# A RetNet front and an MLP-mixer on one core: letting the first front's PSUM tiles come from either of two bank sets

## The chip, the cores and the metric

One core of a Trainium2 chip runs the whole kernel. The metric is the device time of one execution in microseconds (us). Five executions of the kernel before are given by their median; one further execution was profiled.

## The reference

The kernel computes a recurrent retention layer over q, k and v (4 batches, 8 heads, 768 positions, head size 64) and feeds it to an MLP-mixer block with a token part and a channel part.

```python
state = gamma * state + k[:, :, t] (outer) v[:, :, t]      # per batch and head
y[:, :, t] = scale * q[:, :, t] @ state
...
x = y.transpose(0, 2, 1, 3).reshape(B, S, H * D)            # (4, 768, 512)
u = x + (relu(x.T @ w_tok1) @ w_tok2).T                     # w_tok1 (768, 256), w_tok2 (256, 768)
out = u + relu(u @ w_ch1) @ w_ch2                           # w_ch1 (512, 1536), w_ch2 (1536, 512)
```

All inputs and the output are float32; the matmuls run on float16 tiles.

## The kernel before

**Work.** A batch is cut into four *pairs* of heads, p = 0 to 3 (128 of the 512 columns each), and the sequence into six chunks of 128 positions, three to a half. `front(b, p)` makes one pair of one batch, `back(b)` the channel part of one batch. Line numbers are those of the kernel before.

`front(b, p)` records these operations, each with the engine that runs it:

- loads: k as float32 (`kf`, L261), q and v; for batches 0 and 1 on POOL's DMA queue with a cast to float16 (L280, L283, L286), but k of the very first pair on SP's; for batches 2 and 3 all on SP's queue with casts on POOL (L298);
- the scaling of k on DVE (L317); the transposes of k and q on PE (L333, L337, here "Tk" and "Tq") and their copies out of PSUM (L345; kT on DVE and qT on ACT for batch 0); from batch 2 on they are DMA transposes on SP (L352);
- the products of k and v on PE (L366), the running state U on DVE (L375, L378), its scaled copies r on ACT and DVE (L385, L392);
- the scores, half by half (L408 on PE, two PSUM tiles to a half), masked on DVE (L421), or, for pairs 1 to 3 of batch 0 (second head of each), cast on ACT (L419) and masked by a select on POOL (L425);
- the outputs Y (L442 and L445 on PE), scaled into x (L456 on ACT, L460 on DVE) and cast to float16 on POOL (L473) or, for pair 3 of batch 0, directly by ACT;
- the token part: L496 (with wt1), relu on ACT (L504), L517 (with wt2), the addition to x on DVE (L524), the cast to float16 ("u", L535) on POOL, and the transpose of u into uT: on PE and ACT for batch 0 (L548, L557), as a DMA transpose on SP for the others (L571).

`back(b)` runs `ch1` (L604 on PE with wc1, relu L617 on ACT) and `ch2` (L637 on PE with wc2, addition L646 on DVE, store L653 on SP) for each half: 96 L604 and 72 L637 matmuls in a batch (the last tile of the last batch in two parts). An accumulator of ch1 takes four L604, one for each pair.

**Order.** Nothing is scheduled by hand. Every operation is an `Op` with an engine, a priority, an occupancy and a latency in ns, what it depends on, and the buffers (`Slot`) it takes and uses. `arrange()` plays these costs forward: it takes, again and again, the operation that can start first (with ties by priority; PE prefers fronts to backs), and the resulting list is the program order of every engine. The engines then run their lists in order and wait on semaphores. So a buffer that `arrange()` sees as taken moves an operation back in the order, and the order stays even where the buffer comes free earlier on the chip.

**Buffers.** Each `Slot` names one tag, and `BUFS` says how many buffers a tag has. All PSUM tiles are 128 x 512 float32: five with the tag "fa" for the fronts, three with "ba" for the backs. In batch 0 the token part of pairs 0 and 1 (`TOKBA = 2`) uses "ba", which the backs do not need by then; all else of a front uses "fa".

```python
BUFS = dict(kf=4, qf=4, vf=4, k16=3, q16=4, v16=4, kT=4, qT=4, U=3, am=8, x16=2, h1=4, u16=3, u16w=2,
            x=3, uT=3, h2=2, o=3, r16=NR, fa=5, ba=3)
```

**DMA in the plan.** `arrange()` keeps a clock for SP's ring and one for POOL's (`free["SPring"]`, `free["POOLring"]`). After the first 5 us it lets a transfer of SP begin only when POOL's ring is free.

**Zero matmuls.** Where the plan has PE wait before it takes a PSUM tile in batch 0's front, `tile_of` (L198) puts matmuls on a tile of zeros there, as many as fill three quarters of the planned wait. They write into the tile that is being taken.

Of the kernel before, what the change touches and what calls it, by code (L numbers as in the profile page):

```python
# [17 lines left out]
def kernel(  # L18
# [64 lines left out]
    r16 = [const_p.tile([P, NC - 1, P], F16, name=f"r16_{i}") for i in range(NR)]  # L83
    for t in r16:
# [9 lines left out]
    BUFS = dict(kf=4, qf=4, vf=4, k16=3, q16=4, v16=4, kT=4, qT=4, U=3, am=8, x16=2, h1=4, u16=3, u16w=2,  # L94
                x=3, uT=3, h2=2, o=3, r16=NR, fa=5, ba=3)
    SEM, GUARD = 80, 100
# [3 lines left out]
    QLONG = 1200  # L100
    ASIDE, RACT = ((1, 1), (1, 3), (2, 1), (2, 3), (3, 1), (3, 3)), ()
    KPOOL = ()
    FILL, TOKBA, PRE, TWICE, SOFT = 0.75, 2, 2, 1, 2
    ops = []

    class Slot:


        def __init__(self, tag):
            self.tag, self.users, self.tile = tag, [], None  # L110

    class Op:
        def __init__(self, eng, prio, occ, lat, emit, deps=(), takes=(), uses=(), guard=0, dma=0):
# [9 lines left out]
    def arrange():  # L123


        way = {}
        for op in reversed(ops):
            if op.first is not None:
                way[op] = way.get(op, 0) + op.lat + SEM
                for d in op.deps:  # L130
                    way[d] = max(way.get(d, 0), way[op])
        for op in ops:
            if op.first is not None:
                op.prio = (op.prio[0], 0, EARLY * op.first - way[op], op.first)
        free = dict(PE=5700, ACT=5000, DVE=4600, POOL=1100, SP=1300, SPring=1300, POOLring=1300)
        taken = {t: [] for t in BUFS}
        todo, order, ring = list(ops), [], dict(SP=[], POOL=[])
        while todo:
            best = []
            for op in todo:  # L140
                if any(d.end is None for d in op.deps):
                    continue
                start = free[op.eng]
                if op.dma and len(ring[op.eng]) >= RING[op.eng]:
                    start = max(start, ring[op.eng][op.count - 1 - RING[op.eng]])
                for d in op.deps:
                    if d.eng == op.eng and (d.dma or d.eng == "PE"):
                        continue
                    start = max(start, d.end + (30 if d.eng == op.eng else SEM) + op.guard)
                more = {}  # L150
                for s in op.takes:
                    q = taken[s.tag]
                    n = len(q) + more.get(s.tag, 0) - BUFS[s.tag]
                    more[s.tag] = more.get(s.tag, 0) + 1
                    if n >= 0:
                        old = q[n]
                        if any(u.end is None for u in old.users):
                            break
                        start = max([start] + [u.end + SEM for u in old.users])
                else:  # L160
                    best.append((start, op))
            t = min(b[0] for b in best)

            eng = min(best, key=lambda b: (b[0], b[1].prio))[1].eng
            start, op = min((b for b in best if b[1].eng == eng and b[0] <= t + 20),
                            key=lambda b: b[1].prio)
            free[op.eng] = start + op.occ
            op.start = start
            if op.dma:

                mine, other = op.eng + "ring", ("POOL" if op.eng == "SP" else "SP") + "ring"
                at = max(free[mine], start + (op.occ + 200 if op.eng == "POOL" else 50))
                both = max(0, free[other] - at)
                shared = min(op.dma, both // 2)
                if op.eng == "SP" and at > 5000:

                    at, shared = max(at, free[other]), 0
                free[mine] = at + op.dma + shared
                free[other] += shared
                op.end = free[mine] + 1600  # L180
                ring[op.eng] += [op.end if op.eng == "POOL" else free[mine]] * op.count
            else:
                op.end = start + op.lat
            for s in op.takes:
                taken[s.tag].append(s)
            todo.remove(op)
            order.append(op)
        return order
# [33 lines left out]
    def front(b, p):  # L222
        first = b == 0
        g = 0 if first else GUARD
        n = [0]

        def op(eng, occ, lat, emit, deps=(), takes=(), uses=()):
# [95 lines left out]
        KT, QT = Slot("kT"), Slot("qT")  # L323

        def turn(src, dst, dep, eng):
            T = Slot("fa")

            def emit():
                T.tile = tp = tile_of(T, ps, [P, 512], FP).bitcast(F16)
                for c in range(NC):  # L330
                    if src is Q and soft and b < LONG:
                        for j in range(2):
                            nc.tensor.transpose(tp[j * D:(j + 1) * D, c * P:(c + 1) * P],  # L333
                                                src.tile[:, j * NC + c], ident16)
                        continue
                    o = src.tile[:, c] if src is K else src.tile[:, 2 * c:2 * c + 2]
                    nc.tensor.transpose(tp[:, c * P:(c + 1) * P], o.rearrange("p h d -> p (h d)"), ident16)  # L337
            t = op("PE", 340, 500, emit, [dep, t1_done.get(b * NP - 1) if b > 0 else None], [T], [src])

            def emit():  # L340
                d, o = tile_of(dst, sb, [P, S], F16), T.tile[:, :S]
                if dst is QT and b < LONG:
                    d = d.rearrange("d (f p i) -> d f i p", f=2, i=HC)
                    o = o.rearrange("d (f i p) -> d f i p", f=2, i=HC)
                (nc.scalar.copy if eng == "ACT" else nc.vector.tensor_copy)(d, o)  # L345
            occ = dict(ACT=1350 if dst is QT and b < LONG else 700, DVE=470)[eng]
            return op(eng, occ, occ + 90, emit, [t], [dst], [T])

# [8 lines left out]
        qt = crossbar(Q, QT, qc) if b >= XQ else turn(Q, QT, qc, "ACT")  # L357


        ST, US, RS = Slot("fa"), Slot("U"), Slot("r16")  # L360

        def emit():
            st = tile_of(ST, ps, [P, 512], FP)
# [32 lines left out]
        am_ops = []  # L396
        two_before = y_done.get(b * NP + p - 2)
        for hf in range(2):
            A = [Slot("fa"), Slot("fa")]

            def emit(hf=hf, A=A):
                a = [tile_of(A[j], ps, [P, 512], FP).rearrange("p (i t) -> p i t", t=P)
                     for j in range(2)]
                for i in range(HC):
                    t = slice((hf * HC + i) * P, (hf * HC + i + 1) * P)
                    for j in range(2):
                        r = slice(j * D, (j + 1) * D)
                        nc.tensor.matmul(a[j][:, i], KT.tile[r, t], QT.tile[r, t],  # L408
                                         start=True, stop=True)
            a = op("PE", 180, 350, emit, [kt, qt, two_before], A, [KT, QT])  # L410
            for j in range(2):
                off = first and (p, 2 * hf + j) in ASIDE
                M = AM[2 * hf + j]

                def emit(j=j, A=A, off=off, M=M):
                    am = tile_of(M, sb, [P, HC, P], F16)
                    src = A[j].tile.rearrange("p (i t) -> p i t", t=P)
                    if off:
                        nc.scalar.copy(am, src[:, :HC])  # L419
                    else:  # L420
                        nc.vector.tensor_tensor(am, src[:, :HC], mask, ALU.mult)  # L421
                m = op(*(("ACT", 390, 470) if off else ("DVE", 470, 550)), emit, [a], [M], [A[j]])
                if off:
                    def emit(M=M):
                        nc.gpsimd.affine_select(  # L425
                            out=M.tile, in_=M.tile, compare_op=ALU.is_ge, fill=0.0,
                            base=0, pattern=[[0, HC], [1, P]], channel_multiplier=-1)
                    m = op("POOL", 470, 540, emit, [m], [], [M])
                am_ops.append(m)
        X16 = Slot("x16")  # L430
        x_ops, xf = [], []
        for hf in range(2):
            Y = Slot("fa")

            def emit(hf=hf, Y=Y):
                y = tile_of(Y, ps, [P, 512], FP)
                R = RS.tile
# [48 lines left out]
            if not first or p < DIRECT:  # L486
                x_ops.append(op("POOL", 450, 510, lambda e=emit_16: e(False), [ev] + x_ops, tk16, [X] + us16))

        FA = "ba" if first and p < TOKBA else "fa"
        T1, H1 = Slot(FA), Slot("h1")  # L490

        def emit():
            acc = tile_of(T1, ps, [P, 512], FP)
# [4 lines left out]
        t1 = op("PE", 690, 860, emit, x_ops + [wops["t1", 0], None if first else t2_done.get(b * NP + p - 1)], [T1], [X16])  # L498
# [6 lines left out]
        hr = op("ACT", 300, 380, emit, [t1], [H1], [T1])  # L505
        tt, uc = [], None
        wide = b >= XU
        T, UW = Slot(FA), Slot("u16w")
        for hf in range(2):
            T2, U16 = Slot(FA), UW if wide else Slot("u16")  # L510

            def emit(hf=hf, T2=T2):
                acc = tile_of(T2, ps, [P, 512], FP)
# [24 lines left out]
            if wide:  # L538
                continue
            if first:  # L540
                T = Slot(FA)

            def emit(hf=hf, U16=U16, T=T):
                if hf == 0 or first:
# [118 lines left out]
    for p in range(NP):  # L663
        front(0, p)
# [46 lines left out]
```

## Time and profile before

| | us |
|---|---|
| median of 5 runs | 202.94 |
| lowest and highest of them | 201.8 and 203.68 |
| profiled execution | 200.37 |
| its span, first to last instruction | 198.7 |
| PE busy in the span | 191.6 |
| DVE, ACT, POOL busy | 113.5, 92.5, 77.2 |

The span is what the trace covers; 1.7 us of the profiled execution lie around it. The profiled execution was faster than the five by 1.4 us and more, so a sum made from the trace is carried to the median as a difference. The page of the profile gives the span in 40 slices of 5 us: a digit is the share of the slice in which an engine was busy, in tenths. PE counts as busy while matmuls overlap, so its digits say that something was running and not that it ran at its peak. Where a row of a timeline has brackets at its end, the engine was idle before it for so long, and the name in the brackets ended that idle time. A transfer is shown by its issue; the time to its landing is given apart.

### The profile page before, as it was taken

How to read it: one execution, taken by the hardware profiler on the slowest of the kernel's cores; microseconds unless marked ns; L12 is line 12 of the kernel's file. 1: busy time of each engine (PE TensorE's matmuls, PEld its weight loads, DVE VectorE, ACT ScalarE, POOL GpSimd, SP SyncE). 2: the span in 40 equal slices, each digit the busy share in tenths (PEclk: the TensorE clock that was granted, in tenths of full speed). 3: DMA queues.
4: the chain of work that ended last, by engine and by line, in shares of the span. 5: the costliest groups of instructions: out<-in, count | busy, mean ns of one | idle time of the engine just before them, and what ended most of it. 6: DMA issues, size and time to landing. Idle time of an engine off the chain costs nothing.

```text
span 198.7 us, 4693 instructions
## 1 busy us (share of the span) xinstructions
PE 191.6 (96%) x1876; PEld 117.4 (59%) x1876; DVE 113.5 (57%) x285; ACT 92.5 (47%) x207; POOL 77.2 (39%) x124
## 2 busy tenths in 40 slices
PE   7799899999999999999999999999999999999993
PEld 2454796567766555666566655675666545545552
DVE  6699766596489875765885487629762021021021
ACT  7266996886682111284126531553326405504600
POOL 7998899945603621333533333243131000000000
PEclk9999999999999999999999999999999999999999
DMA  6999999999999989999999999999614021012012
GB/s 116 186 216 184 210 223 200 163 205 214 132 168 221 206 216 134 258 258 136 231 224 259 240 180 214 221 235 176 98 62 118 9 101 57 3 53 106 0 53 106
DMA packets 90069, 31.75 MB, mean 160 GB/s; under 512 B 82592, under 2 KB 85920, under 8 KB 90048
## 3 DMA queue, kind: packets, MB, share of 16 engines
q1 hardware_dynamic: 64800, 21.63, 56.5%
q0 software_dynamic: 25248, 9.83, 42.6%
q8 instruction: 14, 0.23, 0.5%
q14 instruction: 7, 0.06, 0.1%
HBM read 26.74 MB, written 6.29 MB: 166 GB/s over the span
## 4 chain that ended last, share of the span: by engine, by line
PE 80%; DMA 8%; POOL 7%; DVE 2%; issue 1%; SPq 0%; POOLq 0%; DVEq 0%
PE ba L637 31%; PE ba L604 28%; DMA wt<-in_moe_w_tok_dram 5%; PE fa L496 4%; PE fa L517 4%; PE fa L408 3%; DMA vf<-in_v_dram 3%; PE fa L445 2%; POOL v L286 2%; PE fa L442 2%; POOL kf L261 2%; PE fa L366 2%; PE fa L337 1%; POOL q L283 1%; POOL u L535 1%
## 5 line engine op out<-in xcount | busy, mean ns | idle before, releaser
L604 PE MATMUL ba<-uT,wc 128*128 128x384 f16 x384 | 69.2, 326 | 0.0
L637 PE MATMUL ba<-wc,h 128*128 128x512 f16 (+1 forms) x300 | 68.1, 371 | 0.0
L617 ACT ACTIVATE h<-ba 128x384 f16<-128x384 f32 x96 | 46.8, 491 | 37.9 <-PE ba L604 37.4
L604 PEld LDWEIGHTS <-wc 128*128 128x128 f16 x384 | 35.4, 98 | 22.1
L637 PEld LDWEIGHTS <-h 128*128 128x128 f16 x300 | 27.6, 98 | 25.7
L646 DVE TENSOR_TENSOR o<-x,ba 128x512 f32<-128x512 f32 (+1 forms) x25 | 16.6, 664 | 40.8 <-PE ba L637 40.7
L421 DVE TENSOR_TENSOR am<-fa,mask 128x384 f16<-128x384 f32 x58 | 30.0, 551 | 3.3 <-PE fa L408 2.8
L473 POOL CAST x<-x 128x384 f16<-128x384 f32 x30 | 15.3, 518 | 26.4 <-issue 17.7
L524 DVE TENSOR_TENSOR x<-x,fa 128x384 f32<-128x384 f32 x28 | 14.7, 551 | 13.1 <-PE fa L517 12.9
L456 ACT ACTIVATE x<-fa,gy 128x192 f32<-128x192 f32 (+1 forms) x42 | 15.0, 424 | 15.2 <-PE fa L445 15.2
L535 POOL CAST u16w<-x 128x384 f16<-128x384 f32 x24 | 11.9, 507 | 25.5 <-DVE x L524 19.9
L378 DVE SCALAR_TENSOR_TENSOR U<-U,gp,fa 128x64 f32<-128x64 f32 x64 | 17.7, 277 | 1.3
L317 DVE TENSOR_SCALAR k<-kf,gk 128x384 f16<-128x384 f32 x32 | 15.2, 517 | 3.7 <-DMA kf<-in_k_dram 3.6
L385 ACT ACTIVATE r<-U 64x320 f16<-64x320 f32 x16 | 7.5, 467 | 17.0 <-DVE U L378 16.9
L504 ACT ACTIVATE h<-fa 128x256 f16<-128x256 f32 x14 | 5.4, 386 | 20.5 <-PE fa L496 20.5
L445 PEld LDWEIGHTS <-am 128*128 128x128 f16 x192 | 12.3, 98 | 3.1 <-DVE am L421 0.2
L445 PE MATMUL fa<-v,am 128*128 128x64 f16 x192 | 13.8, 193 | 0.0
L517 PEld LDWEIGHTS <-wt 128*128 128x128 f16 x192 | 11.9, 98 | 2.6 <-issue 0.2
L198 PE MATMUL fa<-zero 128*128 128x512 f16 x37 | 11.2, 440 | 2.1 <-DVE zero L52 1.3
L496 PEld LDWEIGHTS <-wt 128*128 128x128 f16 x192 | 11.7, 98 | 2.5 <-DMA wt<-in_moe_w_tok_dram 0.6
L442 PE MATMUL fa<-r,qT 128*128 128x128 f16 x80 | 12.2, 220 | 0.0
L517 PE MATMUL fa<-h,wt 128*128 128x128 f16 x168 | 12.0, 219 | 0.0
(61 smaller groups left out, 170.8 us busy)
## 6 DMA issues: line engine op xcount, KB each, us to landing
out_dram<-o SPq DMA_DIRECT2D x23, 256.0 KB, 2.6
kf<-in_k_dram SPq DMA_DIRECT2D x9, 384.0 KB, 5.1
qf<-in_q_dram SPq DMA_DIRECT2D x8, 384.0 KB, 5.1
vf<-in_v_dram SPq DMA_DIRECT2D x8, 384.0 KB, 5.5
kf<-in_k_dram POOLq DMA_DIRECT2D x7, 384.0 KB, 9.4
v<-in_v_dram POOLq DMA_DIRECT2D x8, 192.0 KB, 7.1
wc<-in_moe_w_ch_dram POOLq DMA_DIRECT2D x1, 1536.0 KB, 12.6
wc<-in_moe_w_ch_dram POOLq DMA_DIRECT2D x1, 1024.0 KB, 13.8
```

The lines of the kernel that those rows point to most:

```text
L317: (nc.gpsimd if keng == "POOL" else nc.vector).tensor_scalar(k16[:, :, j, :], src, gk[:, h:h + 1], None, ALU.mult)
L378: nc.vector.scalar_tensor_tensor(U[:, c], U[:, c - 1], gp[:, p:p + 1], o, ALU.mult, ALU.add)
L421: nc.vector.tensor_tensor(am, src[:, :HC], mask, ALU.mult)
L442: nc.tensor.matmul(o, QT.tile[:, c * P:(c + 1) * P], R[:, c - 1], start=True, stop=False)
L445: nc.tensor.matmul(o[:, j * D:(j + 1) * D], AM[2 * hf + j].tile[:, i], V.tile[:, j * NC + c], start=(c == 0), stop=(c == 0 or j == 1))
L473: nc.gpsimd.tensor_copy(X16.tile[:, half(hf)], X.tile[:, half(hf), pc])
L496: nc.tensor.matmul(acc[:, jt * P:(jt + 1) * P], wt1[:, i, jt * P:(jt + 1) * P], X16.tile[:, i], start=(i == 0), stop=(i == NC - 1))
L517: nc.tensor.matmul(acc[:, i * P:(i + 1) * P], wt2[:, jt, t], H1.tile[:, jt], start=(jt == 0), stop=(jt == NJ - 1))
L604: nc.tensor.matmul(acc[:, :SH], w[:, ct, f * P:(f + 1) * P], UT.tile[:, ct, sh * SH:(sh + 1) * SH], start=(ct == 0), stop=(ct == NP - 1))
L617: nc.scalar.activation(H2.tile[:, ft], A.tile[:, :SH], AF.Relu)
L637: nc.tensor.matmul(A.tile[:, :CW], H2.tile[:, ft, i * P:(i + 1) * P], wc2[:, ft, cs], start=(ft == 0), stop=(ft == NF - 1))
L646: nc.vector.tensor_tensor(o[:, :CW], X.tile[:, sh * HC + i, cs], A.tile[:, :CW], ALU.add)
```

## The change

The PSUM tiles of batch 0's fronts may come from "fa" or from "ba". A `Slot` now holds a list of tags, and `arrange()` picks for each tile, at the moment it places the operation, the tag of which a buffer comes free first in the plan (the first named if equal). `FREE = 4` makes this hold for all four pairs of batch 0, in the transposes, the products of k and v, the scores and the outputs Y; in the token part it holds for pairs 0 and 1 (which had "ba" alone), and pairs 2 and 3 keep "fa". Fronts of later batches keep "fa", the backs keep "ba".

A second edit is in the plan's view of the DMA rings: a transfer of SP after the first 5 us no longer waits for all of POOL's ring. It waits only for POOL transfers with a planned length over 1900 ns (the weights), where it would overlap them, and shares time with the others. No DMA is added or removed.

```diff
-    FILL, TOKBA, PRE, TWICE, SOFT = 0.75, 2, 2, 1, 2
+    FREE, FILL, TOKBA, PRE, TWICE, SOFT = 4, 0.75, 2, 2, 1, 2
...
-        def __init__(self, tag):
-            self.tag, self.users, self.tile = tag, [], None
+        def __init__(self, *choice):
+            self.choice, self.tag, self.users, self.tile = choice, None, [], None
...
                 for s in op.takes:
-                    q = taken[s.tag]
-                    n = len(q) + more.get(s.tag, 0) - BUFS[s.tag]
-                    more[s.tag] = more.get(s.tag, 0) + 1
-                    if n >= 0:
-                        old = q[n]
-                        if any(u.end is None for u in old.users):
-                            break
-                        start = max([start] + [u.end + SEM for u in old.users])
+                    when = []
+                    for tag in s.choice:
+                        n = len(taken[tag]) + more.get(tag, 0) - BUFS[tag]
+                        if n < 0:
+                            when.append((0, len(when), tag))
+                        elif all(u.end is not None for u in taken[tag][n].users):
+                            when.append((max(u.end + SEM for u in taken[tag][n].users), len(when), tag))
+                    if not when:
+                        break
+                    at, _, tag = min(when)
+                    start = max(start, at)
+                    more[tag] = more.get(tag, 0) + 1
+                    op.tags.append(tag)
...
                 at = max(free[mine], start + (op.occ + 200 if op.eng == "POOL" else 50))
+                if op.eng == "SP" and at > 5000:
+
+                    for t0, t1 in long:
+                        if at + op.dma > t0:
+                            at = max(at, t1)
                 both = max(0, free[other] - at)
                 shared = min(op.dma, both // 2)
-                if op.eng == "SP" and at > 5000:
-
-                    at, shared = max(at, free[other]), 0
                 free[mine] = at + op.dma + shared
                 free[other] += shared
+                if op.eng == "POOL" and op.dma > 1900:
+                    long.append((at, free[mine]))
...
+        FB = ("fa", "ba") if first and p < FREE else ("fa",)
+        FT = ("fa", "ba") if first and p < TOKBA else ("fa",)
...
-        ST, US, RS = Slot("fa"), Slot("U"), Slot("r16")
+        ST, US, RS = Slot(*FB), Slot("U"), Slot("r16")
...
-            A = [Slot("fa"), Slot("fa")]
+            A = [Slot(*FB), Slot(*FB)]
...
-            Y = Slot("fa")
+            Y = Slot(*FB)
...
-        FA = "ba" if first and p < TOKBA else "fa"
-        T1, H1 = Slot(FA), Slot("h1")
+        T1, H1 = Slot(*FT), Slot("h1")
```

The tile of `turn` becomes `Slot(*FB)` too, and the token part's other tiles become `Slot(*FT)`.

## Prediction

> **What bounds the kernel now.** I read the slices of the page first, then busy time by stretch, then the order of time on PE, POOL and SP.
>
> From the page, then two rows of the busy-time table by stretch (its columns stand in the first line):
>
> ```profile
> PE   7799899999999999999999999999999999999993
> ...
> POOL 7998899945603621333533333243131000000000
> PEclk9999999999999999999999999999999999999999
> ```
>
> ```profile
> core 0: us, PE busy (x) PEld busy (x) DVE busy (x) ACT busy (x) POOL busy (x), PEclk, DMA share, GB/s
> ...
> 22.00:33.00 11.00, 10.66 (x172) 8.91 (x173) 7.02 (x15) 9.75 (x29) 9.78 (x19) 1.00 1.38 214
> ```
>
> There are two regimes. From about 33 us PE is never short: adding matmuls at their spacing (0.163 us for L604, 0.2155 for L637, 0.056 for a 128-column one) gives 162.5 us of work between the first L604 (31.67) and the end of PE (195.5), and the largest gaps between PE rows there are 0.14 to 0.28 us, five in all. Nothing can be won there, only lost; what moves the end is when the front of batch 0 (first 33 us) lets PE start this stream. In the front POOL and ACT, not PE, are full: 9.78 and 9.75 of the last 11 us.
>
> PE in order of time (start, length, row, idle before and its releaser):
>
> ```profile
> 16.49 0.94 PE L408 MATMUL fa<-qT,kT 64*128 64x128 f16 x12
> 17.67 1.89 PE L198 MATMUL fa<-zero 128*128 128x512 f16 x8 [0.25 <-ACT am L419]
> ...
> 22.03 0.84 PE L496 MATMUL ba<-x,wt 128*128 128x128 f16 x12 [0.50 <-DMA wt<-in_moe_w_tok_dram]
> 22.81 0.51 PE L408 MATMUL fa<-qT,kT 64*128 64x128 f16 x12
> 23.25 0.82 PE L198 MATMUL ba<-zero 128*128 128x512 f16 x3
> ...
> 32.78 1.63 PE L604 MATMUL ba<-uT,wc 128*128 128x384 f16 x9
> ```
>
> The first half of pair 2's scores runs with the second half of pair 1's at 16.49; its own second half runs at 22.81, six us later, though qT and kT of pair 2 were there by 16.8. Half a pair's scores take two banks, and five "fa" banks do not reach. PE fills the time with L198 matmuls on zeros. So the bank shortage shows as order, not as waits.
>
> POOL in order of time:
>
> ```profile
> 12.91 0.86 POOL L207 DMA_DIRECT2D wt<-in_moe_w_tok_dram  x1
> 14.07 0.68 POOL L473 CAST x<-x 128x384 f16<-128x384 f32 x1 [0.30 <-ACT x L456]
> ...
> 17.13 0.51 POOL L425 TENSOR_SCALAR_AFFINE_SELECT am<-am 128x384 f16<-128x384 f16 x1 [0.51 <-ACT am L419]
> ...
> 22.78 0.95 POOL L473 CAST x<-x 128x384 f16<-128x384 f32 x2 [0.67 <-ACT x L456]
> ...
> 30.44 2.11 POOL L535 CAST u<-x 128x384 f16<-128x384 f32 x4 [0.35 <-DVE x L524]
> ```
>
> From the issue of wt1 (ends 13.77) to the last u cast (ends 32.55) POOL idles in these four places only, 0.30 + 0.51 + 0.67 + 0.35 = 1.83 us. That is the most a faster front can give as long as POOL's list stays the same.
>
> **The Trainium skill.** "PSUM — Partial Sum Buffer", Specifications (TRN2): eight banks of 2 KiB per partition, out of reach of GpSimd and DMA. The trace agrees on the second: every POOL cast reads and writes SBUF tiles (x<-x), so POOL holds no bank, and the 5 + 3 banks are freed by ACT and DVE. "Perfetto Trace Analysis", Optimizing Tensor Performance: independent groups should rotate through different banks so that evacuation overlaps the next matmuls; the six-us delay above agrees. "TensorE: Matmul & The Clock Gate", What's actually happening: the clock halves after an idle window of about 3.4 us; here it was full in every slice, with 40 zero matmuls as cover. "DMA: Bandwidth & Descriptors", Issuing engines are not separate DMA queues: transfers of SP and POOL interleave on the same 16 engines. So the edit to the planner's ring model changes order only; landings of uT on SP already vary from 2.8 to 7.6 us.
>
> **The change, part by part.** Set beside the old order, the built one shows:
>
> - *Zero matmuls* (L198): 40 become 32. Eight at 0.23 us (10 took 2.32) are 1.8 us of PE, but they stood in waits. I cost them at 0 alone; lower bound 0, upper bound the 1.8. Cover for the clock stays: no stretch of the hand pass leaves PE idle for over 0.7 us.
> - *Scores* (L408): each pair's 12 matmuls now stand together and ahead of the first L496; before, 18 of 48 stood behind it. Follow it by hand, with durations from the rows of before and landing = issue + time to landing. q of pair 1 lands at 4.91 + 5.3 = 10.2. Seven zero matmuls start at 8.45 in a free bank and end at 10.1; Tq1 10.3 to 10.8 (before 11.25), its ACT copy (1.46) ends 12.3, scores 1 at 12.4 (before 14.74 and 16.49). ACT's two casts (0.49 each) end 13.8, so the first POOL select follows the wt1 issue at once. Price: the outputs Y of pair 0 come at 13.3 instead of 12.43 and its x cast at 15.5 instead of 14.07; its reader is L496, which waits for wt1 until 12.91 + 9.1 = 22.0, so this is hidden.
> - Pair 2: q lands 14.05, qT ends 17.2, Y1 waits for r1 on DVE until 16.8, all scores at 17.75. ACT cast done 18.5; POOL is free at 18.1 and idles 0.4. Y2 at 21.2 (before 24.95).
> - Pair 3: q lands 19.06 as before, qT ends 21.5, scores 22.1. The first L496 stands behind them, at 22.75 instead of 22.03: a loss of 0.7 there.
> - From there PE runs L496 2 x 0.67, Y3 0.3, L517 0.67 (its h waits on ACT until 24.85), Y3 0.35, L496 0.67, L517 0.67, and reaches L517 of pair 2 at 28.3. DVE adds (0.56) end 29.35, 29.85, 30.35, 30.85; POOL's last four casts (0.5 each) follow at 29.45 and end at 31.45. A pass with slightly shorter waits on ACT and DVE ended at 31.1.
> - *POOL*: the same casts, selects and DMA issues (17 us of work after wt1), with selects ahead of x casts. kf of batch 1 is issued at 19.5 (before 19.41), so it lands near 33.2 as before. The order puts 27 L604 (4.4 us) ahead of that load's transpose, which before had 12: PE reaches it at 35.6 and does not wait.
> - *SP and POOL ring model*: SP's transfers are now planned to wait for POOL's long ones only. No instruction comes or goes. The first output store moves ahead of the four loads of batch 2 (kf at 54.93 before); it is ready near 58.3, so these loads go 3.4 us later. v of pair 0 lands near 66.1 as the third of them, its cast ends 67, and L366 reads it at 69: cover 2 us, so I cost it at 0; from 0 to +1 if that cover goes.
> - *Later order*: counted from the first L604, batch 1's fronts stand about 2 us of PE work later, ch1 and ch2 about 1.2 us earlier. PE is full either way: 0.
>
> Sum: the stream resumes after the last u cast, at 32.78 before and at 31.35 to 31.7 after, with three L604 done in both: 1.1 to 1.4 us less; I take 1.2. The profiled execution was 200.37 (span 198.7 and 1.7 around it), so it would be 199.2. The median of the five runs is 202.94, 2.6 above that execution; 202.94 - 1.2 = 201.7. Bounds from both sides: at most 1.8 from POOL's idle time; downwards the front may gain nothing, or lose the 0.7 of the later L496.
>
> **Rivals.** A measurement of this kernel can tell about 0.5% (1.0 us) from no change.
>
> *A, the likeliest, 0.58:* the front ends 0.9 to 1.8 us earlier and the stream keeps it: 201.1 to 202.0, mostly more than 0.5%.
>
> *B, 0.24:* the front is held by what does not change (landings of q3 at 19.06 and wt1 at 22.0, POOL full behind them). For: ACT and POOL at 9.8 of 11. Against: POOL's 1.83 us idle. Gain 0 to 0.9: 202.0 to 202.9.
>
> *C, slower, 0.18:* the end of batch 1's front now meets its ch1. Before, on SP:
>
> ```profile
> 73.54 2.76 SPq L571 DMA_TRANSPOSE uT<-u16w  x1
> ```
>
> This last transpose of batch 1 landed 4.7 us after its issue, at 78.24, 7.4 us after its L517 started (70.86). Its first reader came 10.9 us after that start. In the new order between them stand L517 0.67, 22 L637 4.74, L408 0.44, 2 L637 0.43, 6 L604 0.98, Y 0.3 and 3 L604 0.49: 8.05 us. Margin 0.65. If the transpose takes the 7.6 us that another did, PE stalls 2.2 us and the sum is 202.94 - 1.2 + 2.2 = 203.9. It decides from a landing time of 5.4 us.
>
> *The change doesn't do what it says* is ruled out by the order: the second half of pair 0's scores is written to "ba".
>
> **How the numbers follow.** Faster by over 0.5%: most of A, 0.54. Within: B and what is left of A, with a little of C, 0.29. Slower: 0.17. A's own range is 201.1 to 202.0. For eight in ten I reach from 200.5 (POOL's idle time all gone, and some spread of the runs) to 203.7 (most of C).
>
> **What would show it.** Right: the second half of scores 2 near 18 us, fewer L198 rows, last u cast near 31.3, L604 unbroken from 31.6, and end of PE 1.2 us earlier. Wrong: a POOL wait over 0.6 us before a select or u cast (B), or a PE gap over 0.5 us ahead of a single L604 near 78 us with uT named, or ahead of L366 near 69 us (C).

## Result, and the profile after

| | before | after |
|---|---|---|
| median (72 and 37 runs), us | 202.07 | 201.28 |
| lowest and highest, us | 200.35 to 204.17 | 200.11 to 202.65 |
| ratio after / before, 95% interval | | 0.9962, 0.9946 to 0.9977 |
| profiled execution, span, us | 200.37, 198.7 | 200.97, 199.3 |

The change takes 0.77 us off (0.46 to 1.09 from the interval). A second comparison on another occasion gave 0.9941 (0.9917 to 0.9965), which is 1.2 us. All ratios in this text leave out executions over 1.5% above the fastest of their kernel, while the medians are of all, so a ratio is not always the quotient of two medians shown. The two profiled executions stand the other way round, because the one of before happened to be 1.7 us under its own median. So an end of one trace must not be set against an end of the other. What can be compared is a length within a trace, and two lengths are used below. The *front chain* runs from the start of the first scores to where the L604 stream resumes with three of its matmuls done. The *stream* runs from there to the end of PE. PE has the same 1485 matmuls to do from that mark on in both kernels.

In the kernel after, every line number is 12 to 15 higher: L604 is L618, L637 is L651, L408 is L423, L496 is L510, L517 is L531, L198 is L210, L425 is L440, L535 is L549, L366 is L381. In e1 they are 4 lower than in after.

The slices of PE, POOL and the clock, from the page of after:

```profile
PE   7788999999999999999999999999999999999993
...
POOL 7997999913801550244333514243422100000000
PEclk9999999999999999999999999999999999999999
```

The busy-time table of after, for the stretch shown of before:

```profile
core 0: us, PE busy (x) PEld busy (x) DVE busy (x) ACT busy (x) POOL busy (x), PEclk, DMA share, GB/s
22.00:33.00 11.00, 10.39 (x167) 8.82 (x165) 6.87 (x17) 9.32 (x25) 10.97 (x20) 1.00 1.35 213
```

The page shows the full clock in every slice with eight zero matmuls fewer. POOL is now busy for 10.97 of these 11 us (before 9.78): its idle places near 22.8 and 30.4 are gone.

The front chain of before starts at this row of PE:

```profile
7.94 0.51 PE L408 MATMUL fa<-qT,kT 64*128 64x128 f16 x12
```

PE of after in order of time:

```profile
8.39 0.34 PE L423 MATMUL fa<-qT,kT 64*128 64x128 f16 x6
...
17.63 0.23 PE L457 MATMUL fa<-r,qT 128*128 128x128 f16 x1 [0.35 <-DVE r L407]
...
18.36 0.40 PE L423 MATMUL fa<-qT,kT 64*128 64x128 f16 x7
...
22.27 0.39 PE L423 MATMUL fa<-qT,kT 64*128 64x128 f16 x7
...
22.94 0.83 PE L510 MATMUL fa<-x,wt 128*128 128x128 f16 x12
...
32.24 4.06 PE L618 MATMUL ba<-uT,wc 128*128 128x384 f16 x24
```

The scores of pair 2 are all at 18.36 and those of pair 3 all at 22.27. (The other matmuls of each group go to a "ba" tile in between, in rows of their own.) No second half stands behind the token part. The first L510 is at 22.94. The front chain starts at 8.39, so it lasts 32.24 - 8.39 = 23.85 us. In before it was 32.78 - 7.94 = 24.84.

POOL of after:

```profile
19.36 0.99 POOL L440 TENSOR_SCALAR_AFFINE_SELECT am<-am 128x384 f16<-128x384 f16 x2 [1.19 <-ACT am L434]
...
20.54 1.06 POOL L276 DMA_DIRECT2D kf<-in_k_dram  x1 [0.19 <-issue]
...
28.93 2.95 POOL L549 CAST u<-x 128x384 f16<-128x384 f32 x6
```

From the end of the issue of wt1 (13.71) to the last u cast (31.88) it idles in these two places only, 1.19 + 0.19 = 1.38 us. The last six casts stand without a gap.

These lengths for the kernels compared below, in us; "PE idle" is the idle time of PE inside the stream, from the busy-time table. (h3 is left out: nine of its L618 run before the last transposes of u, so the mark is another.)

| kernel | order of the front | first scores | front chain | stream | PE idle |
|---|---|---|---|---|---|
| before | old | 7.94 | 24.84 | 162.65 | 0.12 |
| g1 (before once more) | old | 9.28 | 24.83 | 163.23 | 0.90 |
| e2 (ring edit alone) | old | 9.30 | 25.41 | 164.35 | 1.21 |
| e3 (old order, tiles moved) | old | 8.37 | 24.86 | 163.35 | 0.92 |
| after | new | 8.39 | 23.85 | 163.81 | 0.78 |
| e0 (after once more) | new | 8.20 | 23.35 | 163.99 | 1.01 |
| e1 (banks alone) | new | 9.27 | 23.70 | 163.17 | 0.38 |
| g2 (after, r of pairs 0 to 2 on ACT) | new, edited | 9.30 | 24.06 | 164.03 | 1.06 |
| g3 (after, no zero matmuls in waits) | new, edited | 8.53 | 25.25 | 163.36 | 0.69 |
| g4 (after, pair 2 masked on DVE) | new, edited | 8.08 | 23.26 | 163.06 | 0.25 |
| h4 (the same once more) | new, edited | 8.47 | 23.68 | 163.00 | 0.25 |
| h2 (e1, pair 2 masked on DVE) | new, edited | 8.87 | 23.51 | 163.40 | 0.26 |
| h1 (before, pair 2 masked on DVE) | old, edited | 8.52 | 25.33 | 164.54 | 1.79 |

The first scores move by 1.4 us between executions, and the front moves with them. Each row is one execution: equal programs (before and g1, after and e0, g4 and h4) differ by up to 0.5 us in the chain, 0.6 in the stream and 0.8 in PE's idle time.

### The profile page after: what moved, and what is told of

Same layout as the page of the kernel before. It is cut to its first block, busy times and chain, and to the rows that moved or that the text cites. A ratio compares the mean times of both kernels' runs of the same rounds, so it can differ in the third digit from the quotient of the medians.

```text
span 199.3 us, 4681 instructions
## 1 busy us (share of the span) xinstructions
PE 190.6 (96%) x1868; PEld 116.5 (58%) x1868; DVE 112.2 (56%) x285; ACT 92.4 (46%) x207; POOL 76.5 (38%) x124
## 3 DMA queue, kind: packets, MB, share of 16 engines
q0 software_dynamic: 25248, 9.83, 40.9%
## 4 chain that ended last, share of the span: by engine, by line
PE 70%; DMA 10%; DVE 8%; issue 4%; POOL 4%; SPq 2%; ACT 1%; POOLq 0%
PE ba L618 29%; PE ba L651 25%; PE fa L510 3%; PE fa L531 3%; DMA vf<-in_v_dram 3%; DMA v<-in_v_dram 3%; DMA qf<-in_q_dram 3%; PE fa L423 2%; DMA qT<-q 2%; DVE am L436 2%; DVE U L393 2%; SPq L367 2%; PE fa L460 2%; PE fa L381 1%; DVE k L332 1%
## 5 line engine op out<-in xcount | busy, mean ns | idle before, releaser
L618 PE MATMUL ba<-uT,wc 128*128 128x384 f16 x384 | 69.6, 326 | 0.0
L651 PE MATMUL ba<-wc,h 128*128 128x512 f16 (+1 forms) x300 | 68.0, 371 | 0.0
L618 PEld LDWEIGHTS <-wc 128*128 128x128 f16 x384 | 35.6, 98 | 21.8
L651 PEld LDWEIGHTS <-h 128*128 128x128 f16 x300 | 27.5, 98 | 26.6
L436 DVE TENSOR_TENSOR am<-fa,mask 128x384 f16<-128x384 f32 x55 | 28.1, 551 | 4.4 <-PE fa L423 4.2
L538 DVE TENSOR_TENSOR x<-x,fa 128x384 f32<-128x384 f32 x31 | 16.2, 550 | 9.3 <-PE fa L531 9.3
L549 POOL CAST u16w<-x 128x384 f16<-128x384 f32 x24 | 12.0, 515 | 23.7 <-DVE x L538 23.4
L471 ACT ACTIVATE x<-fa,gy 128x192 f32<-128x192 f32 (+1 forms) x34 | 12.5, 423 | 17.8 <-PE fa L460 17.8
L393 DVE SCALAR_TENSOR_TENSOR U<-U,gp,fa 128x64 f32<-128x64 f32 x56 | 15.6, 278 | 1.3
L332 DVE TENSOR_SCALAR k<-kf,gk 128x384 f16<-128x384 f32 x32 | 13.9, 477 | 4.1 <-DMA kf<-in_k_dram 4.1
L531 PE MATMUL fa<-h,wt 128*128 128x128 f16 x186 | 13.2, 219 | 0.0
L531 PEld LDWEIGHTS <-wt 128*128 128x128 f16 x192 | 11.8, 98 | 2.0
L510 PEld LDWEIGHTS <-wt 128*128 128x128 f16 x192 | 11.7, 98 | 2.0
L510 PE MATMUL fa<-x,wt 128*128 128x128 f16 x180 | 12.5, 219 | 0.0
L460 PE MATMUL fa<-v,am 128*128 128x64 f16 x174 | 12.5, 193 | 0.0
L313 POOL CAST q<-qf 128x768 f16<-128x768 f32 x8 | 6.6, 827 | 15.0 <-DMA qf<-in_q_dram 15.0
```

The lines of the kernel that those rows point to most:

```text
L332: (nc.gpsimd if keng == "POOL" else nc.vector).tensor_scalar(k16[:, :, j, :], src, gk[:, h:h + 1], None, ALU.mult)
L393: nc.vector.scalar_tensor_tensor(U[:, c], U[:, c - 1], gp[:, p:p + 1], o, ALU.mult, ALU.add)
L460: nc.tensor.matmul(o[:, j * D:(j + 1) * D], AM[2 * hf + j].tile[:, i], V.tile[:, j * NC + c], start=(c == 0), stop=(c == 0 or j == 1))
L510: nc.tensor.matmul(acc[:, jt * P:(jt + 1) * P], wt1[:, i, jt * P:(jt + 1) * P], X16.tile[:, i], start=(i == 0), stop=(i == NC - 1))
L531: nc.tensor.matmul(acc[:, i * P:(i + 1) * P], wt2[:, jt, t], H1.tile[:, jt], start=(jt == 0), stop=(jt == NJ - 1))
L538: nc.vector.tensor_tensor(xo, xo, T2.tile[:, :HC * P].rearrange("p (i d) -> p i d", d=P), ALU.add)
```

## Experiments

Each ratio is to runs of before in the same comparison, with its 95% interval. Before had medians of 202.53 (e0 to e3), 202.65 (g1 to g4) and 202.12 us (h1 to h4).

### The changed kernel once more

**e0**, after without any edit.

> The changed kernel once more, on the same chip as the three beside it. Theory (the front frees the stream about 0.6 us earlier and the rest is level): 0.4 to 1.1 us under the kernel before. In the trace the last u cast ends near 31.9 us and L618 runs unbroken from 32.2. Whether the small PE gaps after 80 us of the first profile (0.2 to 0.4 us each, some 2 us together) come again tells whether they belong to the kernel or to one execution.

Measured: 201.36 us, 0.9941 (0.9917 to 0.9965), a little more than expected. The last u cast ends at 31.19 and the stream resumes at 31.55, both earlier than expected. Of the small gaps of PE after 80 us only one stands in both traces, ahead of L381 at 85.9, so most of them belong to one execution. Its POOL waits less before pair 2's selects than the first trace of after did:

```profile
18.68 0.99 POOL L440 TENSOR_SCALAR_AFFINE_SELECT am<-am 128x384 f16<-128x384 f16 x2 [0.71 <-ACT am L434]
```

### The banks alone

**e1**, after with the old view of the DMA rings:

```diff
                 at = max(free[mine], start + (op.occ + 200 if op.eng == "POOL" else 50))
-                if op.eng == "SP" and at > 5000:
-
-                    for t0, t1 in long:
-                        if at + op.dma > t0:
-                            at = max(at, t1)
                 both = max(0, free[other] - at)
                 shared = min(op.dma, both // 2)
+                if op.eng == "SP" and at > 5000:
+
+                    at, shared = max(at, free[other]), 0
                 free[mine] = at + op.dma + shared
                 free[other] += shared
-                if op.eng == "POOL" and op.dma > 1900:
-                    long.append((at, free[mine]))
```

> The choice of banks alone, with the old view of the DMA rings in the plan. Its front is the changed kernel's, instruction for instruction up to the middle of ch1 of batch 0; only the later order differs. Theory: the gain is the front's, so this has all of it, 0.4 to 1.1 us under the kernel before, and its last u cast ends near 31.9. Rival 1 (the ring edit brings the gain): within 0.3 us of the kernel before. Rival 2 (the ring edit gives part of the front's gain back by loads planned too late): 1.2 us or more under it.

Measured: 201.64 us, 0.9934 (0.9899 to 0.9969), and a front chain of 23.70. The front is that of after, instruction for instruction on PE (the first 678 matmuls). So the shorter chain comes with the banks. In time, e1 and e0 can't be told apart. The gain, 1.3 us, lies in the range of the second rival (the ring edit gives part back), and the stream of e1 is 163.17 where after and e0 have 163.8 and 164.0; the times don't settle it.

### The ring edit alone

**e2**, before with only the reverse of the hunk above (the list `long` and the loop over it).

> The new view of the DMA rings alone, with the banks as before. Its front is the kernel's before, instruction for instruction up to the middle of ch1 of batch 0. Theory: level with the kernel before, within 0.4 us, last u cast near 32.5. Rival 1: 0.5 to 1 us faster. Rival 2: 0.5 us or more slower, with PE gaps ahead of L366 and L408 of batches 2 and 3.

Measured: 203.15 us, 1.0019 (0.9984 to 1.0054). The front has the old order (the first 676 matmuls are those of before) and the stream is the second longest of the table, 164.35 with 1.21 us of PE idle. No gain of the edit by itself is seen. A loss of up to 0.5% isn't excluded, and isn't shown either.

### The banks free, the order kept

**e3**: `arrange()` places everything as in before. After that, each tile of batch 0's front, its token part apart, gets the tag whose oldest buffer ends first in the plan, so PE and SP run the old lists with all eight banks:

```diff
+        held = dict(fa=[], ba=[])
+        for i, op in enumerate(order):
+            for s in op.takes:
...
+                for tag in (("fa", "ba") if s.free else (s.tag,)):
...
+                s.tag = min(when)[2]
+                held[s.tag].append(s)
         return order
```

> The order of the kernel before, unchanged on every engine; only then each PSUM tile of batch 0's front is given the bank, of either set, that the plan has free first. So the waits on banks go and the order stays. Theory (the shortage showed as order, not as waits; PE waited 0.8 us in all on evacuations there, filled or covered): level with the kernel before, within 0.3 us, last u cast 32.3 to 32.6. Rival (the waits themselves were the cost): 0.4 us or more faster, last u cast before 32.1.

Measured: 201.89 us, 0.9966 (0.9944 to 0.9988). The interval lies below one, where an effect of the order alone would leave the time as it was; but the kernel before, run again as g1, gave 0.9979. Nor does the time tell e3 from e0 in the same comparison (201.89 and 201.36 us, with intervals that overlap), and the change itself gave 0.9962 in its first comparison. Only e0 and e1 together, 29 executions with one front, lie under e3: by 0.5 us in the mean, 0.2 to 0.9 as an estimate made by resampling the times on record. The trace is clearer than the time (L427 is L408 here and L624 is L604):

```profile
8.37 0.34 PE L427 MATMUL fa<-qT,kT 64*128 64x128 f16 x6
...
33.23 1.63 PE L624 MATMUL ba<-uT,wc 128*128 128x384 f16 x9
```

The front chain is 24.86 (before 24.84), although PE no longer waits for ACT or DVE to empty a bank ahead of zero matmuls. So in this trace free banks without a new order don't shorten the front. A gain of some tenths elsewhere isn't excluded.

### The kernel before as its own control

**g1**, before without any edit.

> The kernel before, entered as if it were a changed one: a second profile of its front, and what a comparison of equal kernels gives. Ratio 1 within 0.3%. Theory (a front runs as one chain from the landing of the first v to the last u cast, and executions shift the whole chain): from the start of the first scores to the resumed L604 stream it takes 24.8 to 25.5 us, as in the first profile (24.84), whatever the landing; the changed kernel's took 23.4 to 23.9 in three profiles. Rival (the first profile of before was a lucky one in the chain itself): over 25.6.

Measured: 202.27 us, 0.9979 (0.9955 to 1.0003). Equal programs differ here by 0.2%; g4 and h4 below, equal too, differ by 0.6%. Its trace shows how the front of one program moves:

```profile
9.00 0.35 PE L366 MATMUL fa<-v,k 128*64 128x64 f16 x10 [1.62 <-DMA v<-in_v_dram]
```

The first v landed 6.1 us after its issue, where the other profiled executions show 4.6 to 5.7. PE waits for it, and the chain from the first scores to the last u cast (33.88) is later than in the first profile of before by 1.3 us. The length of the chain, 24.83, is that of before.

### r of pairs 0 to 2 on ACT

Y of pair 1 waits for r on DVE (the row at 17.63 above). **g2** takes r off DVE:

```diff
-    ASIDE, RACT = ((1, 1), (1, 3), (2, 1), (2, 3), (3, 1), (3, 3)), ()
+    ASIDE, RACT = ((1, 1), (1, 3), (2, 1), (2, 3), (3, 1), (3, 3)), (0, 1, 2)
```

> The changed kernel with the second scaled copy of the state (r, 0.48 us each) of pairs 0, 1 and 2 of the first front moved from DVE to ACT. Theory DVE (with banks free, DVE has no idle time from the first state copy to the last r, 8.5 to 24.4 us, and sets the front): DVE loses 1.4 us of work there, scores 2 and 3 come 0.5 to 1 us earlier, and the kernel is 0.3 to 1 us faster than the changed one. Theory POOL (POOL's list is the bound and its 1.2 us wait before the select of pair 2 an accident of order): the last u cast moves by less than 0.3 us and the time is within 0.3 us of the changed kernel. Rival (ACT takes the bound over): slower by 0.3 us or more, with POOL waiting longer on ACT's casts.

Measured: 202.89 us, 1.0019 (0.9999 to 1.004): the gain of the change is lost. POOL waits for ACT at its first select and for DVE before pair 2's:

```profile
14.81 0.52 POOL L440 TENSOR_SCALAR_AFFINE_SELECT am<-am 128x384 f16<-128x384 f16 x1 [1.15 <-ACT am L434]
...
19.84 0.52 POOL L440 TENSOR_SCALAR_AFFINE_SELECT am<-am 128x384 f16<-128x384 f16 x1 [1.40 <-DVE k L332]
```

Little of the first wait is ACT's new work. The execution had a slow start (see the last section), as that of e1 had, and in e1 the first select waits 0.94 us for ACT without the edit. PE no longer waits for r, and pair 2's scores come 8.90 us after the first scores (9.83 in e1); yet POOL's next wait is 1.40 us (1.18 in e1), and the chain is 24.06 (23.70 in e1). So taking DVE's wait away did not shorten the front. These 0.4 us don't explain a loss of over 1 us; where the rest goes is open.

### Without the fill of zero matmuls

**g3** leaves out the 23 zero matmuls that the plan puts into waits and keeps the nine at the start:

```diff
-    FREE, FILL, TOKBA, PRE, TWICE, SOFT = 4, 0.75, 2, 2, 1, 2
+    FREE, FILL, TOKBA, PRE, TWICE, SOFT = 4, 0.0, 2, 2, 1, 2
```

> The changed kernel without the zero matmuls inside the front; only the nine at the start stay (32 become 9). Theory: they stood in waits and cost nothing, and PE's clock stays full without them, since no idle stretch of PE is long: within 0.3 us of the changed kernel. Rival 1 (they delay real matmuls that are ready): 0.3 to 1 us faster. Rival 2 (the clock falls in the thinner front): slower by 0.5 us or more, and the clock row of the page shows it below 0.9 in some slice of the first 35 us.

Measured: 202.48 us, 1.0024 (1.0 to 1.0048), so 0.6% to 0.8% above the changed kernel. The busy-time table of g3, in the columns shown above, shows what happened:

```profile
5.00:10.00 5.00, 2.04 (x41) 1.38 (x40) 2.33 (x8) 1.44 (x1) 4.99 (x6) 0.89 1.57 181
10.00:15.00 5.00, 3.44 (x48) 2.64 (x49) 4.82 (x13) 2.58 (x4) 4.78 (x7) 0.50 1.69 215
15.00:20.00 5.00, 4.24 (x63) 3.56 (x62) 4.33 (x14) 3.68 (x8) 3.39 (x6) 0.50 1.65 188
```

After 5 us in which PE was busy for 2.04, the granted clock is half for 10 us, although PE is busy for 69% and then 85% of them. The longest idle time before a matmul there is about 1.5 us:

```profile
10.52 0.85 PE L348 MATMUL ba<-ident,q 128*64 128x128 f16 x12 [1.47 <-DMA q<-in_q_dram]
```

Twelve transposes take 0.85 us instead of 0.53, and the chain is 25.25. So the 23 zero matmuls in the waits are worth over 1 us. That the clock makes all of it is likely but not shown: 20 of the 22 executions list a mean clock of 0.963 to 0.975, and the two that list 1.0 took 202.38 and 202.68 us, no less than the others.

### Pair 2 masked on DVE

POOL's largest wait in after is for pair 2's scores, cast on ACT. **g4** lets DVE mask all of pair 2, so POOL has two selects and ACT two casts fewer:

```diff
-    ASIDE, RACT = ((1, 1), (1, 3), (2, 1), (2, 3), (3, 1), (3, 3)), ()
+    ASIDE, RACT = ((1, 1), (1, 3), (3, 1), (3, 3)), ()
```

> The changed kernel with pair 2's two cast-and-select masks (ACT 0.49, POOL 0.5 each) done by DVE instead (0.55 each). It takes away what POOL waited 1.2 us for. Theory POOL: POOL's list is 1 us shorter and its wait is gone, the last u cast comes 0.7 us or more earlier, and the kernel is 0.4 us or more faster than the changed one. Theory DVE: DVE gets 1.1 us more where it has no idle time, scores 3 and the first L496 come later, and the kernel is level with the changed one or up to 0.8 us slower.

Measured: 200.22 us, 0.9888 (0.9862 to 0.9915), the fastest of all, from six executions. **h4** is the same kernel in another comparison.

> The changed kernel with pair 2's masks on DVE once more, beside the others: 1.8 to 2.8 us under the kernel before, with the chain from the first scores to the resumed L618 stream at 23.0 to 23.5 us.

Measured: 200.88 us, 0.9946 (0.9904 to 0.9989), less gain than expected and a ratio like that of the change alone (e0, 0.9941). So a gain of the edit over the change is seen in g4's comparison only. Where it was seen, it didn't come for the reason expected. POOL of g4:

```profile
18.86 0.50 POOL L488 CAST x<-x 128x384 f16<-128x384 f32 x1 [0.96 <-ACT x L471]
...
19.69 1.05 POOL L276 DMA_DIRECT2D kf<-in_k_dram  x1 [0.33 <-DVE am L436]
...
29.10 2.01 POOL L549 CAST u<-x 128x384 f16<-128x384 f32 x4 [0.52 <-DVE x L538]
```

The wait for ACT's cast is gone and three others stand there, 1.81 us in sum. The front chain is 23.26 and 23.68, close to what after shows without the edit (23.35 and 23.85). What differs in both traces is the stream: 163.0 instead of 163.9, and 0.25 us of PE idle instead of 0.78 and 1.01. Where PE idles in e0, and which cast it waits for:

```profile
85.95 0.35 PE L381 MATMUL fa<-v,k 128*64 128x64 f16 x10 [0.63 <-POOL v L313]
```

In after, POOL in turn waits for the load of this v, the one of pair 1 of batch 2:

```profile
85.05 0.83 POOL L313 CAST v<-vf 128x768 f16<-128x768 f32 x1 [2.56 <-DMA vf<-in_v_dram]
```

SP issues that load at 80.38 in after, but at 72.36 in g4:

```profile
80.38 0.58 SPq L276 DMA_DIRECT2D vf<-in_v_dram  x1
```

```profile
72.36 0.70 SPq L276 DMA_DIRECT2D vf<-in_v_dram  x1
```

In g4 the cast of v ends at 79.35 and PE needs it at 80.68. In after it ends at 85.88 and PE starts at 85.93, as soon as it can. PE starts within 0.1 us of the end of the v cast at four places in after, at two in before and in g1, and at none in g4 and h4. So the other masks change the plan of batches 2 and 3, and with it how early v is loaded: 41.0 us after the mark in g4 and 48.1 in after. That the time follows from this isn't shown: no kernel moved only that load, and g2 loads this v early too (41.7 us after the mark) with a stream of 164.03.

### The same edit on the old banks

**h1**, before with the edit of g4.

> The kernel before (banks and rings as before) with pair 2's two cast-and-select masks done by DVE. Theory (two steps: banks first, then POOL; with the old order pair 2's second scores come only behind the first L496, so POOL has other work while it waits for them, and taking its selects away frees less): 0 to 0.8 us under the kernel before, and at least 1 us over the changed kernel with the same edit. Rival (the edit of the masks is worth its 2 us by itself, whatever the banks): 1.5 us or more under the kernel before.

Measured: 203.89 us, 1.0108 (1.0057 to 1.016): clearly slower. Before the last u casts POOL waits for DVE:

```profile
31.61 1.51 POOL L535 CAST u<-x 128x384 f16<-128x384 f32 x3 [1.18 <-DVE x L524]
```

The chain is 25.33 and PE idles 1.79 us in the stream. With the old banks the pair's masks come late, just ahead of DVE's additions. That they make the whole loss isn't shown: before the last four additions DVE itself had been idle for 1.64 us and waited for PE's L517.

**h2**, e1 with the edit of g4.

> The choice of banks alone (old view of the rings in the plan) with pair 2's masks on DVE. Its front is that of the changed kernel with this edit. Theory (the ring edit is level or costs a little by PE gaps in batches 1 to 3): 2 to 3 us under the kernel before, level with or up to 0.6 us faster than the same with the ring edit. Rival (the ring edit gains in this company): 0.5 us or more slower than it.

Measured: 200.67 us, 0.9944 (0.9905 to 0.9984), less gain than expected. The edit costs 1.1% with the old banks; with the new ones the time is about that of e1 (0.9934). With the ring edit (h4, 0.9946) it is the same, so what the masks add to the ring edit isn't told apart here.

### Pairs 2 and 3 masked on DVE

**h3**, after with `ASIDE` cut to `((1, 1), (1, 3))`.

> The changed kernel with the masks of pairs 2 and 3 on DVE; only pair 1 keeps cast and select. Theory POOL (POOL's list before the last u cast sets the end of the front): two more selects of 0.5 us go, and the last u cast comes up to 1 us earlier than with pair 2 alone on DVE: 2.5 to 3.3 us under the kernel before. Rival (DVE takes the bound over, since the last pair's masks stand right before its additions): the same as with pair 2 alone, or slower by up to 1 us.

Measured: 201.81 us, 0.9995 (0.9945 to 1.0045): no gain over before is left. POOL waits for DVE before its last u casts:

```profile
31.31 0.97 POOL L549 CAST u<-x 128x384 f16<-128x384 f32 x2 [1.53 <-DVE x L538]
```

DVE isn't the bound there, however. It had been idle for 1.80 us before these additions and waited for PE's L531. In this order PE takes transposes of u ahead of that L531 and waits for POOL's cast at one of them (0.47 us at 28.51).

## Why the prediction was right, and what was mis-sized

The forecast was 1.2 us faster by mechanism A, and 0.77 (0.46 to 1.09) came; the second comparison gave 1.2. By its size, 0.77 lies in rival B's range (0 to 0.9) and not in A's (0.9 to 1.8). That 201.28 us lies in A's range of times is partly luck: the forecast started from a median of 202.94 for before, and 72 executions gave 202.07. What speaks for A is the chain inside the traces. Step by step:

- *Order, not waits: right for the chain.* e3 frees the banks and keeps the order, and its chain stays at 24.86; e1 has the new order, and 23.70. In device time e3 itself stands 0.7 us under before, so a part of the gain may come from the free banks without the order; that g1, without any edit, stands at 0.9979 shows how much of it can be chance.
- *The front ends 1.1 to 1.4 us earlier: right as a length.* The chain predicted was 31.35 to 31.7 less 7.94, so 23.4 to 23.8. After, e0 and e1 show 23.85, 23.35 and 23.70, mean 23.63. Before, g1 and e2 have the old order with a mean of 25.03. That is 1.4 us, or 1.2 without e1 and e2, whose scores ran slowly (last section). Of the signs named, the last u cast near 31.3 and the stream from 31.6 came in e0 (31.19 and 31.55) and not in the first trace of after (31.88 and 32.24). An end of PE 1.2 us earlier came in neither trace.
- *The hand pass: nearly right, with one term mis-sized.* The first L510 was put at 22.75 and came at 22.94. Pair 2's scores were put at 17.75 and came at 18.36, since r on DVE, taken as ready at 16.8, held Y1 until 17.63; DVE has no idle time from 8.49 to 24.38. So POOL's wait of 0.4 before pair 2's select was 1.19 in after, 0.71 in e0 and 1.18 in e1. By the prediction's own mark (over 0.6) this was to speak for B. It did not decide: the waits near 22.8 and 30.4 went at the same time.
- *POOL's idle time as the cap (1.83): too narrow a reading.* It was taken from one execution with an early front. In g1, the same program, POOL idles in five places, 1.86 + 0.49 + 0.69 + 0.26 + 0.23 = 3.53 us, because wt1 is issued at a fixed time and the x cast comes with the front. The cap held for quick executions only.
- *Zero matmuls at 0: no cost is seen* for the eight that go, though no run puts them back alone. Their cover for the clock was argued from the Trainium skill ("TensorE: Matmul & The Clock Gate", What's actually happening), with an idle window of about 3.4 us. Read as one unbroken idle time, this doesn't fit g3: the clock halved with no idle time over some 1.5 us. The measurement decides, and the remaining cover is needed.
- *"Later order: 0" and the ring model "0 to +1", both taken at 0: too small, by how much is open.* With a chain 1.2 to 1.4 us shorter and a gain of 0.77 to 1.2, up to 0.6 us was given back. The stream of after and e0 is 163.9, that of before and g1 162.9 (means), 1 us more; but before and g1, equal programs, are 0.6 apart. The traces point to the ring edit. With it the unedited fronts have streams of 163.81, 163.99 (new) and 164.35 (old); without it 163.17 (new) and 162.65, 163.23, 163.35 (old). The times of e0, e1 and e2 don't settle it.
- *The later loads: seen, under the wrong heading, and not shown to be the cost.* In after the first store does move ahead of batch 2's loads, and v of its first pair is issued 29.4 us after the mark, where before has 25.6; 3.4 us later was predicted. The prediction put this to the ring edit. That edit alone (e2) gives 26.4, and the new order without it (e1) 28.5, so most of it comes with the order. In after the cast of this v ends at 70.65 and PE needs it at 70.99, so the cover of 2 us shrank to 0.34. One pair later, PE starts the products of k and v as soon as the cast ends (85.93). But the kernel before stands no better there. Its trace g1:

```profile
85.26 0.35 PE L366 MATMUL fa<-v,k 128*64 128x64 f16 x10 [0.44 <-POOL v L298]
```

- *PE has nothing to win in the stream: not quite.* The gaps of 0.14 to 0.28 us in before are no idle time of PE, which is 0.12 us in all; but g1 idles 0.90 us in its stream, as much as after.
- *Rival C: closer than predicted, and kept off partly by luck.* The way of PE from the L531 of that pair to the first reader of its uT was right: 8.15 us (predicted 8.05). But SP issues this last transpose of batch 1 at 76.46, 4.3 us after the start of that L531, where before has 2.7. It landed in 3.83 us, at 80.29, and its reader, whose turn had just come, started at 80.33. In e0 it took 4.04 us and PE idled 0.12 for it. In g3 it was issued at 78.20 and took 4.4 us, and PE waited for it for 0.69 us, until 82.67. So a wait starts below 3.9 us of landing time and not at 5.4; the 4.7 us of before would have cost almost 1 us (an estimate from these).

## What to carry to other kernels

Where a planner or a fixed order sees a buffer as taken, a shortage can show as a late instruction and not as a wait; look for halves of one step that stand far apart, and free the buffer before the order is made. Compare kernels by lengths inside a trace, from an anchor that both share, since a single execution can be over 1 us early or late; profile an equal program again before reading a few tenths, since these lengths differ by up to 0.6 us as well. When the front of a full stream gets shorter, check the loads and transposes deeper in the stream: here the cover of one v fell from 2 us to 0.34 and that of one uT to nothing. Test a second edit alone: the traces point to the ring edit for what the stream gave back.

## What the hardware showed that was not expected

The granted clock of PE was 0.50 from 10 to 20 us after a stretch with 41% busy time and no idle time over about 1.5 us (g3, above). The landing of the same first load of v took 4.6 to 6.1 us from one execution to the next. PE can also be slow at the start of one execution and not of another. The first twelve transposes of PE in e1, and then in after, which have the same front:

```profile
6.04 0.85 PE L344 MATMUL fa<-ident,q 128*64 128x128 f16 x12 [0.77 <-DMA q<-in_q_dram]
```

```profile
5.99 0.53 PE L348 MATMUL fa<-ident,q 128*64 128x128 f16 x12 [0.74 <-DMA q<-in_q_dram]
```

They start together and take 0.85 against 0.53 us; the transposes of k that follow start at 7.65 against 6.88, and the scores at 9.27 against 8.39. e2 and g2 show the slow ones too (0.85), and g4 has 0.81 with quick matmuls behind. The clock row of the page has a 9 in these slices of e1 all the same, so a slow start has to be read from the lengths of the rows. That it is the clock is likely, since g3's transposes took the same 0.85 us at a granted clock of 0.50; what decides it was not found.
